# Pool's early block sums started by semaphore in VectorE's one-input stretches, with two splits and the late additions moved

## The chip, the cores and the metric

One Trainium2 chip, one core. The metric is the device time of one execution of the program, in microseconds (us). The core has five engines that run their own instruction streams and wait for one another by semaphores: TensorE (PE in the profile; its weight loads are PEld), VectorE (DVE), ScalarE (ACT), GpSimd (POOL) and SyncE (SP, whose queue issues the DMAs). SBUF is the on-chip memory, PSUM the accumulators that TensorE writes.

## The reference

A gated linear attention over 4 batches, 8 heads, 768 tokens and head size 48, followed by a mixture of 8 experts whose token weights are balanced by eight rounds of row and column scaling:

```
f = 1 / (1 + exp(-f_logit))
for t in range(768):
    state = f[:, :, t, :, None] * state + outer(k[:, :, t], v[:, :, t])
    y[:, :, t] = q[:, :, t] @ state
x = y as (3072, 384)
P = exp(x @ w_gate - max)
for _ in range(8):
    P /= P.sum(1) + 1e-09;  P /= P.sum(0) + 1e-09;  P *= 3072 / 8
out = sum over e of P[:, e] * (relu(x @ w1[e]) @ w2[e])      # 384 -> 1024 -> 384
```

## The kernel before

**Splits.** Every fp32 matrix is split into two fp16 parts, a high part (rounded by ScalarE) and a low part (the rest, by VectorE or Pool), and a product is three fp16 matmuls.

**Attention.** The work is cut into 24 items of 128 tokens, six for each batch; an item holds all heads on 112 partitions and 512 columns (8 blocks of 64 tokens). `item(i)` is a Python generator, and each `yield` ends a step. In each step the loop in `fast` lets every live item do its next piece and then lets TensorE do a fixed amount of filler work. A new item begins every 8 steps, so two items overlap. An item loads q, k and f (tile `q`) and v, and does in this order: a sigmoid (L728), a backward scan `r` (L735), the product of k with r (L750, two fp32 inputs in SBUF), the low part of v (`vlc`, L751), a forward scan (L753; one input `ft` in SBUF, the other, `pi`, in PSUM), its product with q on Pool (L760), the split of k (`kb`, L763 and L771) and of the q side (`qh` on ScalarE, L769; `ql` on Pool, L776), a DMA transpose of `kb`, the score matmuls `aps`, the masked scores `am` (L808) and their split `ah` (L814), `al` (Pool, L823), the state `st` and its split `sh` (L822), `sl` (L830, two inputs in SBUF), and the output matmuls `yps`, which read ah, al, qh, ql, sh and sl. The output is split into the token tiles `xh` and `xl`.

**The filler.** Between these pieces TensorE runs experts 0 and 1 directly on finished token tiles: `hps` (first layer), `hh`/`hl` (its split after the relu: ScalarE L470 or L423, VectorE L473 or L424), `yps` (second layer), `yr` (copy out, L494 or L441, then a store).

**The block sums.** After attention the other experts run in a scheme with 15 block products for each period; it needs sums of 128x256 blocks of x. For each batch a list of jobs does this: three additions x = xh + xl (kind V, L986), 17 block sums on Pool (P, L1000), three maxima (V, L1003), two copies (A, L1008), five high parts (H, `xah`/`xbh`, L1016) and five low parts (L, `xal`/`xbl`, L1021). For batches 0 and 1 the jobs run early, inside the items, by `hook`: from item 8 on for batch 0 and from item 15 on for batch 1, at most one VectorE job ahead of the forward scan, up to five Pool and copy jobs behind `td` (L756), and up to two high parts behind `al`. For batches 2 and 3 `convert` runs them beside the balancing of the token weights (`sinkhorn`: tiny VectorE steps, L140 to L172, with matmuls `sk_t`, `sk_m` and `sk_c` between).

**What sets the order.** `pin` chains the instructions of each engine in the order of the code, and `mm` does so for TensorE, so an engine never overtakes a waiting instruction. DMAs on the SP queue are placed by the scheduler.

Of the kernel before, what the change touches and what calls it, by code (L numbers as in the profile page):

```python
# [12 lines left out]
AF = mybir.ActivationFunctionType  # L13
ALU = mybir.AluOpType
# [21 lines left out]
SS = 2.0 ** -11  # L36
# [72 lines left out]
FIRSTAT = ((0,), (0,), (0, 4), (0, 7), (1, 9), (5, 10))  # L109
SECONDAT = ((16, 17), (18, 20), (17, 18), (17, 21), (20, 21), (20, 22), (24, 24), (24, 25))  # L110
CONVSTEP = (30,)
EARLY = {0: 8, 1: 15}
POOL_SUMS = 5
PUTOFF = 17
X_BY_POOL = ()
# [171 lines left out]
def fast(ctx, tc, qkf, vbd, wg, w1, w2, out, flag):  # L287
    nc = tc.nc
# [427 lines left out]
    def item(i):  # L716
# [32 lines left out]
        km = k.rearrange("r (n t) -> r n t", t=C)  # L749
        pin(nc.vector.scalar_tensor_tensor(out=km, in0=km, scalar=KS, in1=r3, op0=ALU.mult, op1=ALU.mult))  # L750
        pin(nc.vector.scalar_tensor_tensor(out=vlc, in0=vr, scalar=VS, in1=vhc, op0=ALU.mult, op1=ALU.subtract))  # L751
        hook(i, 'VL', 1)
        pin(nc.vector.tensor_tensor_scan(out=fl, data0=ft[:, 0:L], data1=pi.rearrange("r n t -> r (n t)"), initial=0.0, op0=ALU.mult, op1=ALU.add))  # L753
        if i == 3:
            pin(nc.vector.tensor_tensor(out=fl, in0=fl, in1=q, op=ALU.mult))
        pin(nc.gpsimd.tensor_tensor(out=td, in0=td, in1=r3[:, :, 0], op=ALU.mult))  # L756
        hook(i, 'PA', POOL_SUMS)
        yield
        if i > 3:
            pin(nc.gpsimd.tensor_tensor(out=fl, in0=fl, in1=q, op=ALU.mult))  # L760
# [5 lines left out]
        ql = ap.tile([R, L], F16, name=f"ql_{i}", tag="ql")  # L766
        for o, rs in vl:
            pin(nc.scalar.activation(out=o, in_=vlc[rs], func=AF.Copy))
        pin(nc.scalar.activation(out=qh, in_=fl, func=AF.Copy))  # L769
        for rs, ks in heads:  # L770
            pin(nc.gpsimd.tensor_tensor(out=kb[rs, 1, :, ks], in0=km[rs], in1=kb[rs, 0, :, ks], op=ALU.subtract))  # L771
        yield
        kt = ktb[i % 2][:, 0:2 * NB * R].rearrange("p (n r) -> p n r", r=R)
        nc.sync.dma_start_transpose(out=kt, in_=kb.rearrange("r n c s -> r (n c) s"))
        yield
        pin(nc.gpsimd.tensor_tensor(out=ql, in0=fl, in1=qh, op=ALU.subtract))  # L776
        yield from wait(4)
        st = ap.tile([R, CT, NP, D], F32, name=f"st_{i}", tag="st")
        td3 = td.rearrange("r (p c) -> r p c", c=CT)
        if s:  # L780
# [46 lines left out]
            pin(nc.vector.tensor_tensor(out=carry[b, s + 1], in0=kvps[1][0:R], in1=st[:, 1], op=ALU.add))  # L827
        yield
        for (o, rs), (hi, _) in zip(sl, sh):
            pin(nc.vector.scalar_tensor_tensor(out=o, in0=sf[rs], scalar=SS, in1=hi, op0=ALU.mult, op1=ALU.subtract))  # L830
        yield
        yield
        if not s:
# [145 lines left out]
    def jobs(b, pools):  # L979
        xqp, alloc, x32 = pools(b)  # L980
        eng = nc.gpsimd if b in X_BY_POOL else nc.vector
        xh, xl = xt[b]
        kept = {}

        def add(k):
            pin(eng.tensor_tensor(out=x32[k], in0=xh[:, k].rearrange("p u t -> p (u t)"), in1=xl[:, k].rearrange("p u t -> p (u t)"), op=ALU.add))  # L986

        def block(v):
            if isinstance(v, str):
                q = int(v[1])  # L990
                return x32[q // 3].rearrange("p (u t) -> p u t", u=2)[:, :, 128 * (q % 3):128 * (q % 3) + 128]
            n = XPOS.index(v)
            return kept['s'][n // 9][:, n % 9, :].rearrange("p (u t) -> p u t", u=2)

        def total(i):
            if not i:
                kept['b'] = [xqp.tile([128, 6, 256], F16, name=f"xb{n}{b}") for n in "hl"]
                kept['s'] = alloc()
            r, p, op, q = XSUMS[i]
            pin(nc.gpsimd.tensor_tensor(out=block(r), in0=block(p), in1=block(q), op=ALU.add if op == '+' else ALU.subtract))  # L1000

        def most(k):
            pin(nc.vector.tensor_reduce(out=xmx[:, b, k:k + 1], in_=x32[k], axis=AX.X, op=ALU.max, apply_absolute_value=True))  # L1003

        def one(n):
            r, q, sign = XONE[n]
            for src, dst in zip((xh, xl), kept['b']):
                pin(nc.scalar.activation(out=dst[:, 4 + n, :].rearrange("p (u t) -> p u t", u=2), in_=src[:, q // 3, :, 128 * (q % 3):128 * (q % 3) + 128], func=AF.Copy, scale=sign))  # L1008

        PIECES = [(0, 0, 3), (0, 3, 6), (0, 6, 9), (1, 0, 2), (1, 2, 4)]  # L1010

        def high(i):
            if not i:
                kept['a'] = [xp.tile([128, 9, 256], F16, name=f"xa{n}{b}", tag=f"x{n}{b}", bufs=1) for n in "hl"]
# [54 lines left out]
    def early_pools(b):
        x32 = [raw_tile(f"x32_{b}_{k}") for k in range(KT)]  # L1070
# [36 lines left out]
    for n in range(8):  # L1107
        at_steps(second[n], 4 + n, *SECONDAT[n])
    begin = {LEADS + STEPS * (i - 3): i for i in range(3, NT)}
    while live or g < max(begin):  # L1110
        if g == 2:
            third = early_item(2)
            go(third)
        if g == 6:
            go(third)
        if g == 9:
            live.append(third)
        if g + 4 in begin:
# [509 lines left out]
```

## Time and profile before

| | |
|---|---|
| time, median of 3 runs | 1482.09 us (1480.91 to 1482.21) |
| profiled execution | 1482.9 us, of it the span 1481.1 us |
| PE busy | 1442.2 us (97% of the span) |
| DVE, ACT, POOL busy | 1254.7, 1110.7, 1082.5 us |
| mean granted TensorE clock | 0.994 |

The items run from the start to about 370 us, the balancing to about 435 us, and the periods of block products fill the rest. PE's busy time can hide a slow clock: a matmul at half clock is busy twice as long. So two things are read together: the waits in front of PE's instructions, and the granted clock of each stretch.

### The profile page before, as it was taken

The numbers are of one execution on the slowest core, as the hardware profiler recorded it, in microseconds if no ns is written. First come the engines' busy times: TensorE is split into PE (matmuls) and PEld (weight loads), VectorE is DVE, ScalarE is ACT, GpSimd is POOL, SyncE is SP. The second block draws the span as 40 slices with busy tenths as digits, with TensorE's granted clock in tenths as the row PEclk, the third lists the DMA queues.
The fourth block names the chain that finished last, engine by engine and source line by source line (L and its number), as shares of the span: only waits on it lengthen the run. The fifth ranks groups of instructions, "written<-read, shape, count | busy, mean of one in ns | idle before, by whom it ended". The sixth has DMA issues, their size and how long they took to land.

```text
span 1481.1 us, 40831 instructions
## 1 busy us (share of the span) xinstructions
PE 1442.2 (97%) x16193; PEld 1268.5 (86%) x16193; DVE 1254.7 (85%) x2569; ACT 1110.7 (75%) x2492; POOL 1082.5 (73%) x1286
## 2 busy tenths in 40 slices
PE   7999999989999999999999999999999999999997
PEld 5778876656557999999999999999999999999996
DVE  8867888986687998899989888888888888888886
ACT  7767768676437778888888888888777777778774
POOL 3344664653454669999999999999888888888873
PEclk9999999999999999999999999999999999999999
DMA  8344435461101012222111111111000000000201
GB/s 261 89 107 128 121 96 126 106 153 49 49 22 60 12 29 61 61 56 60 53 49 58 55 42 47 50 55 50 23 23 23 23 23 23 12 21 14 81 7 67
DMA packets 82809, 90.53 MB, mean 61 GB/s; under 512 B 49872, under 2 KB 69456, under 8 KB 82608
## 3 DMA queue, kind: packets, MB, share of 16 engines
q1 hardware_dynamic: 82176, 87.25, 21.1%
q8 instruction: 128, 2.10, 0.6%
q14 instruction: 73, 0.60, 0.1%
q10 hardware_dynamic: 432, 0.59, 0.1%
HBM read 64.03 MB, written 14.16 MB: 53 GB/s over the span
## 4 chain that ended last, share of the span: by engine, by line
PE 73%; DVE 4%; ACT 0%; issue 0%; DVEq 0%; ACTq 0%
PE kyps L315 29%; PE kb_A L315 9%; PE kb_B L315 9%; PE kb_D L315 6%; PE kxps L315 5%; PE kb_C L315 4%; PE yps L315 4%; PE hps L315 3%; PE kb_E L315 2%; PE kb_F L315 2%; DVE x L986 0%; DVE k1l L1173 0%; DVE hl L424 0%; DVE acc L1329 0%; DVE xal L1021 0%
## 5 line engine op out<-in xcount | busy, mean ns | idle before, releaser
L315 PEld LDWEIGHTS <-k1h 128*128 128x128 f16 x3000 | 282.5, 98 | 21.9 <-issue 2.3
L315 PE MATMUL kyps<-k2h,kgh 128*128 128x192 f16 x1200 | 295.2, 246 | 1.5 <-ACT kyps L1326 1.5
L315 PE MATMUL kyps<-k2h,kgl 128*128 128x192 f16 x1200 | 295.2, 246 | 0.0
L315 PE MATMUL kyps<-k2l,kgh 128*128 128x192 f16 x1200 | 295.2, 246 | 0.0
L315 PEld LDWEIGHTS <-kgh 128*128 128x128 f16 x2400 | 220.9, 98 | 8.5 <-issue 1.8
L1501 POOL TENSOR_TENSOR kgl<-kf,kgh 128x512 f16<-128x512 f32 x147 | 197.3, 1342 | 2.1 <-ACT kgh L1498 2.1
L1329 DVE SCALAR_TENSOR_TENSOR yy<-kyps,pes,part 128x192 f32<-128x192 f32 x270 | 111.4, 413 | 94.6 <-PE kyps L315 84.3
L1501 POOL TENSOR_TENSOR kgl<-kr,kgh 128x512 f16<-128x512 f32 x147 | 174.1, 1184 | 9.6 <-PE kyps L315 8.2
L1368 POOL TENSOR_TENSOR acc<-acc,yy 128x384 f32<-128x384 f32 x135 | 135.0, 1000 | 57.7 <-DVE yy L1329 57.7
L315 PEld LDWEIGHTS <-k1l 128*128 128x128 f16 x1500 | 146.8, 98 | 17.1
L315 PEld LDWEIGHTS <-kh 128*128 128x128 f16 x1200 | 112.7, 98 | 8.4 <-issue 1.8
L315 PEld LDWEIGHTS <-kgl 128*128 128x128 f16 x1200 | 117.4, 98 | 0.1
L315 PE MATMUL yps<-w2h,hh 128*128 128x384 f16 x336 | 111.4, 332 | 5.0 <-ACT hh L470 3.1
L315 PE MATMUL yps<-w2h,hl 128*128 128x384 f16 x336 | 111.6, 332 | 2.3 <-DVE hl L473 2.2
L315 PE MATMUL yps<-w2l,hh 128*128 128x384 f16 x336 | 111.4, 332 | 0.6 <-DVE w2l L388 0.6
L315 PEld LDWEIGHTS <-w1h 128*128 128x128 f16 x1248 | 87.9, 98 | 27.8 <-issue 2.7
L315 PEld LDWEIGHTS <-hh 128*128 128x128 f16 x672 | 65.8, 99 | 44.4 <-ACT hh L470 3.9
L1452 ACT ACTIVATE cp<-kb_A 128x512 f32<-128x512 f32 x150 | 89.8, 599 | 18.1 <-DVE kb_A L1454 15.5
L1326 ACT ACTIVATE kyps<-kyps 128x192 f32<-128x192 f32 x150 | 48.2, 321 | 67.8 <-PE kyps L315 65.7
L1498 ACT ACTIVATE kgh<-kf 128x512 f16<-128x512 f32 x150 | 94.9, 633 | 0.5 <-DVE kf L1475 0.4
L1498 ACT ACTIVATE kgh<-kr 128x512 f16<-128x512 f32 x150 | 94.3, 628 | 0.0
L1478 POOL TENSOR_TENSOR kr<-kr 128x256 f32<-128x256 f32 x100 | 75.9, 759 | 22.6 <-ACT kr L1467 20.4
(320 smaller groups left out, 5382.5 us busy)
## 6 DMA issues: line engine op xcount, KB each, us to landing
q<-in_qkf_dram SPq DMA_DIRECT2D x23, 672.0 KB, 5.4
k1r<-in_w_dram SPq DMA_DIRECT2D x26, 384.0 KB, 3.0
k2r<-in_w_dram SPq DMA_DIRECT2D x26, 384.0 KB, 3.0
ys<-yr SPq DMA_DIRECT2D x48, 192.0 KB, 2.3
yb<-ys SPq DMA_DIRECT2D x48, 192.0 KB, 2.3
vr<-in_vbd_dram SPq DMA_DIRECT2D x24, 192.0 KB, 2.5
out_dram<-acc SPq DMA_DIRECT2D x21, 192.0 KB, 1.9
w1r<-in_w_dram SPq DMA_DIRECT2D x8, 384.0 KB, 7.4
```

The lines of the kernel that those rows point to most:

```text
L315: ins = (nc.tensor.transpose if transpose else nc.tensor.matmul)(**kw)
L1326: pin(nc.scalar.activation(out=out, in_=in_, func=AF.Copy, **kw))
L1329: pin(nc.vector.scalar_tensor_tensor(out=y, in0=ps, scalar=p, in1=z, op0=ALU.mult, op1=ALU.add))
L1368: pin(nc.gpsimd.tensor_tensor(out=y, in0=y, in1=z.rearrange("p s d -> p (s d)"), op=ALU.add))
L1452: pin(nc.scalar.activation(out=fresh(ev[2]), in_=bk, func=AF.Copy))
L1478: pin((nc.gpsimd if ev[2] == 'P' else nc.vector).tensor_tensor(out=r[:, 0], in0=r[:, 1], in1=r[:, 0], op=ALU.subtract))
L1498: pin(nc.scalar.activation(out=hs['g', t][0][i], in_=hs['f' if i else 'r', t], func=AF.Copy))
L1501: pin((nc.vector if tag == str(PERIODS - 1) else nc.gpsimd).tensor_tensor(out=hs['g', t][1][i], in0=hs['f' if i else 'r', t], in1=hs['g', ...
```

## The change

Four edits. (1) The first Pool sum of a hook gets a semaphore dependency on a VectorE instruction (`turn`): in front of the forward scan one sum waits for the last VectorE instruction ahead of that scan; up to three jobs (P, A or V) move behind `sl`, the first sum of them waiting for the last `sl`. The maxima move there too. (2) `qh` is issued one step later, behind the transpose DMA, and `ql` one step later; the score matmuls stay in their step. (3) The additions of batches 2 and 3 (now kind X) take one step each. (4) Batch 1 starts its early jobs at item 16, and what is left of the early jobs runs two at a time in the steps after the last item has begun its second half.

```
--- before.py
+++ after.py
@@ -109,7 +109,7 @@
 FIRSTAT = ((0,), (0,), (0, 4), (0, 7), (1, 9), (5, 10))
 SECONDAT = ((16, 17), (18, 20), (17, 18), (17, 21), (20, 21), (20, 22), (24, 24), (24, 25))
 CONVSTEP = (30,)
-EARLY = {0: 8, 1: 15}
+EARLY = {0: 8, 1: 16}
 POOL_SUMS = 5
 PUTOFF = 17
 X_BY_POOL = ()
@@ -749,12 +749,13 @@
         km = k.rearrange("r (n t) -> r n t", t=C)
         pin(nc.vector.scalar_tensor_tensor(out=km, in0=km, scalar=KS, in1=r3, op0=ALU.mult, op1=ALU.mult))
         pin(nc.vector.scalar_tensor_tensor(out=vlc, in0=vr, scalar=VS, in1=vhc, op0=ALU.mult, op1=ALU.subtract))
-        hook(i, 'VL', 1)
+        hook(i, 'XVL', 1)
+        turn = last.get(mybir.EngineType.DVE)
         pin(nc.vector.tensor_tensor_scan(out=fl, data0=ft[:, 0:L], data1=pi.rearrange("r n t -> r (n t)"), initial=0.0, op0=ALU.mult, op1=ALU.add))
         if i == 3:
             pin(nc.vector.tensor_tensor(out=fl, in0=fl, in1=q, op=ALU.mult))
         pin(nc.gpsimd.tensor_tensor(out=td, in0=td, in1=r3[:, :, 0], op=ALU.mult))
-        hook(i, 'PA', POOL_SUMS)
+        hook(i, 'PA', 1, turn)
         yield
         if i > 3:
             pin(nc.gpsimd.tensor_tensor(out=fl, in0=fl, in1=q, op=ALU.mult))
@@ -766,15 +767,16 @@
         ql = ap.tile([R, L], F16, name=f"ql_{i}", tag="ql")
         for o, rs in vl:
             pin(nc.scalar.activation(out=o, in_=vlc[rs], func=AF.Copy))
-        pin(nc.scalar.activation(out=qh, in_=fl, func=AF.Copy))
         for rs, ks in heads:
             pin(nc.gpsimd.tensor_tensor(out=kb[rs, 1, :, ks], in0=km[rs], in1=kb[rs, 0, :, ks], op=ALU.subtract))
         yield
         kt = ktb[i % 2][:, 0:2 * NB * R].rearrange("p (n r) -> p n r", r=R)
         nc.sync.dma_start_transpose(out=kt, in_=kb.rearrange("r n c s -> r (n c) s"))
+        pin(nc.scalar.activation(out=qh, in_=fl, func=AF.Copy))
+        yield
         yield
         pin(nc.gpsimd.tensor_tensor(out=ql, in0=fl, in1=qh, op=ALU.subtract))
-        yield from wait(4)
+        yield from wait(3)
         st = ap.tile([R, CT, NP, D], F32, name=f"st_{i}", tag="st")
         td3 = td.rearrange("r (p c) -> r p c", c=CT)
         if s:
@@ -827,7 +829,8 @@
             pin(nc.vector.tensor_tensor(out=carry[b, s + 1], in0=kvps[1][0:R], in1=st[:, 1], op=ALU.add))
         yield
         for (o, rs), (hi, _) in zip(sl, sh):
-            pin(nc.vector.scalar_tensor_tensor(out=o, in0=sf[rs], scalar=SS, in1=hi, op0=ALU.mult, op1=ALU.subtract))
+            turn = pin(nc.vector.scalar_tensor_tensor(out=o, in0=sf[rs], scalar=SS, in1=hi, op0=ALU.mult, op1=ALU.subtract))
+        hook(i, 'PAV', 3, turn)
         yield
         yield
         if not s:
@@ -997,7 +1000,10 @@
                 kept['b'] = [xqp.tile([128, 6, 256], F16, name=f"xb{n}{b}") for n in "hl"]
                 kept['s'] = alloc()
             r, p, op, q = XSUMS[i]
-            pin(nc.gpsimd.tensor_tensor(out=block(r), in0=block(p), in1=block(q), op=ALU.add if op == '+' else ALU.subtract))
+            ins = pin(nc.gpsimd.tensor_tensor(out=block(r), in0=block(p), in1=block(q), op=ALU.add if op == '+' else ALU.subtract))
+            if gated[0]:
+                tc.add_manual_dep(ins.ins, gated[0].ins.name, mybir.DependencyInfo(mybir.DependencyClass.Sync, mybir.DependencyReason.DATA), reason="port turn")
+                gated[0] = None
 
         def most(k):
             pin(nc.vector.tensor_reduce(out=xmx[:, b, k:k + 1], in_=x32[k], axis=AX.X, op=ALU.max, apply_absolute_value=True))
@@ -1023,7 +1029,7 @@
                 xc[b] = [[(kept['a'] if n < 9 else kept['b'])[q][:, n % 9, :] for n in range(PRODUCTS)] for q in range(2)]
 
         for k in range(KT):
-            yield 'V', lambda k=k: add(k)
+            yield 'X', lambda k=k: add(k)
         for i in range(len(XSUMS)):
             yield 'P', lambda i=i: total(i)
             if i in (1, 5, 9):
@@ -1041,7 +1047,7 @@
             while kind == 'H' and raw_left() > 0:
                 yield
             job()
-            if kind in 'PL':
+            if kind in 'PLX':
                 yield
 
     class Early:
@@ -1057,14 +1063,16 @@
                 self.next = next(self.jobs, None)
                 most -= 1
 
-    early = {}
-
-    def hook(i, kinds, most):
+    early, gated = {}, [None]
+
+    def hook(i, kinds, most, after=None):
+        gated[0] = after
         for b, first in EARLY.items():
             if i >= first:
                 if b not in early:
                     early[b] = Early(b)
                 early[b].run(kinds, most)
+        gated[0] = None
 
     def early_pools(b):
         x32 = [raw_tile(f"x32_{b}_{k}") for k in range(KT)]
@@ -1107,6 +1115,7 @@
     for n in range(8):
         at_steps(second[n], 4 + n, *SECONDAT[n])
     begin = {LEADS + STEPS * (i - 3): i for i in range(3, NT)}
+    begin_tail = max(begin) + 17
     while live or g < max(begin):
         if g == 2:
             third = early_item(2)
@@ -1125,9 +1134,12 @@
         put_off[0] = g < PUTOFF
         fill([n for at_, n in FILL if g >= at_][-1])
         go_all(g)
+        if g > begin_tail:
+            for run in early.values():
+                run.run('AHLVP', 2)
         g += 1
     for run in early.values():
-        run.run('AHLPV', 99)
+        run.run('AHLPVX', 99)
     actx.close()
     xq = ctx.enter_context(tc.tile_pool(name="xq", bufs=1, reuse_waits="tile"))
     accp = ctx.enter_context(tc.tile_pool(name="accp", bufs=B, reuse_waits="tile"))
```

TensorE's instructions stand in the same order before and after. Pool's order at items 12 and 13, `q_12` and `q_13` being the items' q tiles and `xs` the block sums, before:

```order
L771 TENSOR_TENSOR kb_124<-q_12_3630,kb_124 48x8x64 x2
L776 TENSOR_TENSOR ql_3938<-q_12_3630,qh_3937 112x512
L823 TENSOR_TENSOR al_4011<-am_3977,ah_4010 128x512
L756 TENSOR_TENSOR tds<-tds,r_4058 112x8
L1000 TENSOR_TENSOR xs_0_3208<-x_0_0_2603,x_0_2_2605 128x256
L1000 TENSOR_TENSOR xs_0_3207<-xs_0_3207 128x256
L1000 TENSOR_TENSOR xs_0_3208<-x_0_2_2605,x_0_0_2603 128x256
L1000 TENSOR_TENSOR xs_0_3207<-xs_0_3207 128x256
L1000 TENSOR_TENSOR xs_0_3207<-xs_0_3207,x_0_0_2603 128x256
L760 TENSOR_TENSOR q_13_3944<-q_13_3944 112x512
```

and after, at the same place:

```order
L771 TENSOR_TENSOR kb_124<-q_12_3625,kb_124 48x8x64 x2
L825 TENSOR_TENSOR al_4006<-am_3971,ah_4005 128x512
L778 TENSOR_TENSOR ql_3933<-q_12_3625,qh_3932 112x512
L1003 TENSOR_TENSOR xs_0_3207<-x_0_1_2604,xs_0_3207 128x256
L1003 TENSOR_TENSOR xs_0_3207<-x_0_0_2603,x_0_1_2604 128x256
L757 TENSOR_TENSOR tds<-tds,r_4057 112x8
L1003 TENSOR_TENSOR xs_0_3207<-x_0_0_2603,x_0_1_2604 128x256
L761 TENSOR_TENSOR q_13_3938<-q_13_3938 112x512
```

Ahead of item 13's product with q (L760, now L761) stands one sum instead of five, behind its `td` (L756, now L757); two others stand ahead of `td`, behind `ql`, and `al` of the item before stands ahead of `ql`. ScalarE's order in item 12, before:

```order
L768 ACTIVATE vl_140<-vlc_3767 64x8x48 x2
L769 ACTIVATE qh_3937<-q_12_3630 112x512
L470 ACTIVATE hh_2_1_0_3959<-hps_2_1_0_3851 128x512
L470 ACTIVATE hh_2_1_1_4004<-hps_2_1_1_3963 128x512
L814 ACTIVATE ah_4010<-am_3977 128x512
```

and after:

```order
L769 ACTIVATE vl_140<-vlc_3768 64x8x48 x2
L470 ACTIVATE hh_2_1_0_3953<-hps_2_1_0_3846 128x512
L775 ACTIVATE qh_3932<-q_12_3625 112x512
L470 ACTIVATE hh_2_1_1_3999<-hps_2_1_1_3957 128x512
L816 ACTIVATE ah_4005<-am_3971 128x512
```

`qh` has moved behind the filler's `hh` of the next unit. VectorE's order in the balancing, where batch 3's additions (`x_3`) stand, before:

```order
L172 TENSOR_TENSOR pe<-pe,sk_cs 128x192
L1173 SCALAR_TENSOR_TENSOR k1l_0_7700<-k1s_0_7613,k1h_0_7699 128x640
L986 TENSOR_TENSOR x_3_7743<-xh_5948,xl_5949 128x768 x3
L159 TENSOR_REDUCE pe<-pe 128x24
L160 TENSOR_SCALAR sk_rs<-pe 128x24
L161 RECIPROCAL sk_rs<-sk_rs 128x24
L1173 SCALAR_TENSOR_TENSOR k1l_0_7700<-k1s_0_7613,k1h_0_7699 128x640
L163 TENSOR_TENSOR pe<-pe,sk_rs 128x192
L164 TENSOR_REDUCE sk_cs<-pe 128x8
```

and after:

```order
L172 TENSOR_TENSOR pe<-pe,sk_cs 128x192
L1185 SCALAR_TENSOR_TENSOR k1l_0_7700<-k1s_0_7608,k1h_0_7699 128x640
L989 TENSOR_TENSOR x_3_7743<-xh_5941,xl_5942 128x768
L159 TENSOR_REDUCE pe<-pe 128x24
L160 TENSOR_SCALAR sk_rs<-pe 128x24
L161 RECIPROCAL sk_rs<-sk_rs 128x24
L1185 SCALAR_TENSOR_TENSOR k1l_0_7700<-k1s_0_7608,k1h_0_7699 128x640
L989 TENSOR_TENSOR x_3_7743<-xh_5941,xl_5942 128x768
L163 TENSOR_TENSOR pe<-pe,sk_rs 128x192
L164 TENSOR_REDUCE sk_cs<-pe 128x8
```

One addition instead of three stands between the scaling of `pe` (L172) and the row sums (L159, one line in both), and a second one between the reciprocal (L161) and L163.

## Rows read from the trace of the kernel before

**Rows 1.** The page, busy time of each engine.
```profile
PE 1442.2 (97%) x16193; PEld 1268.5 (86%) x16193; DVE 1254.7 (85%) x2569; ACT 1110.7 (75%) x2492; POOL 1082.5 (73%) x1286
```
**Rows 2.** Waits of PE, 74 to 480 us: total, times, longest.
```profile
PE yps L315 <- ACT hh L470: 2.9, 2, 2.7
PE sk_c L315 <- DVE sk_cs L164: 2.4, 2, 2.1
PE yps L315 <- POOL al L823: 2.2, 2, 1.1
PE yps L315 <- DVE hl L473: 2.0, 5, 0.7
PE lps L315 <- DVE am L808: 2.0, 3, 1.1
PE yps L315 <- ACT hh L423: 1.6, 1, 1.6
PE sk_t L315 <- DVE sk_sm L140: 1.4, 1, 1.4
PE sk_m L315 <- DVE sk_r L146: 0.9, 1, 0.9
...
```
**Rows 3.** Two windows: PE, PEld, DVE, ACT, POOL busy, granted clock, DMA, GB/s.
```profile
190.00:200.00 10.00, 7.13 (x56) 4.18 (x54) 7.23 (x17) 5.30 (x12) 6.41 (x7) 0.83 0.58 138
420.00:430.00 10.00, 7.92 (x40) 4.16 (x39) 9.66 (x22) 2.18 (x6) 7.67 (x12) 0.83 0.13 41
```
**Rows 4.** Groups (74 to 360 us: busy, mean ns | idle), then timeline rows (start, duration).
```profile
L750 DVE SCALAR_TENSOR_TENSOR q<-q,r 112x512 f32<-112x512 f32 x19 | 30.1, 1585 | 0.0
...
L753 DVE TENSOR_TENSOR_SCAN q<-ft,pib 112x512 f32<-112x512 f32 x19 | 22.9, 1208 | 0.0
...
142.57 0.67 DVE L750 SCALAR_TENSOR_TENSOR q<-q,r 112x512 f32<-112x512 f32 x1
...
199.59 3.97 DVE L750 SCALAR_TENSOR_TENSOR q<-q,r 112x512 f32<-112x512 f32 x1
...
202.27 0.74 POOL L1000 TENSOR_TENSOR xs<-xs,x 128x256 f32<-128x256 f32 x1
```
**Rows 5.** Timeline, a forward scan with Pool sums beside it.
```profile
157.44 1.21 DVE L753 TENSOR_TENSOR_SCAN q<-ft,pib 112x512 f32<-112x512 f32 x1
157.59 0.72 POOL L1000 TENSOR_TENSOR xs<-x,x 128x256 f32<-128x256 f32 x1 [2.10 <-DVE x L986]
```
**Rows 6.** Timeline of ScalarE in front of PE's longest wait.
```profile
191.52 0.63 ACT L769 ACTIVATE qh<-q 112x512 f16<-112x512 f32 x1 [1.38 <-POOL q L760]
...
192.17 1.08 ACT L470 ACTIVATE hh<-hps 128x512 f16<-128x512 f32 x2
```
**Rows 7.** Timeline of Pool, `ql` of one item and `al` of the item before.
```profile
311.50 1.35 POOL L776 TENSOR_TENSOR ql<-q,qh 112x512 f16<-112x512 f32 x1
312.81 1.47 POOL L823 TENSOR_TENSOR al<-am,ah 128x512 f16<-128x512 f32 x1
```
**Rows 8.** Timeline of ScalarE, two high parts of batch 1.
```profile
324.95 1.58 ACT L1016 ACTIVATE xah<-xs 128x768 f16<-128x768 f32 x2
```
**Rows 9.** Timeline of VectorE in the balancing.
```profile
382.33 2.68 DVE L986 TENSOR_TENSOR x<-xh,xl 128x768 f32<-128x768 f16 x3
...
419.56 2.69 DVE L986 TENSOR_TENSOR x<-xh,xl 128x768 f32<-128x768 f16 x3
```
**Rows 10.** Timeline of `al`, `sl` and PE's reading of `sl` in two items.
```profile
195.86 1.29 DVE L830 SCALAR_TENSOR_TENSOR sl<-st,sh 48x384 f16<-48x384 f32 x2 [0.65 <-ACT sh L822]
...
201.31 0.40 PE L315 MATMUL yps<-qh,sl 112*128 112x64 f16 x8
...
239.95 1.16 POOL L823 TENSOR_TENSOR al<-am,ah 128x512 f16<-128x512 f32 x1
240.23 2.08 DVE L830 SCALAR_TENSOR_TENSOR sl<-st,sh 48x384 f16<-48x384 f32 x2 [0.20 <-ACT sh L822]
...
242.62 0.40 PE L315 MATMUL yps<-qh,sl 112*128 112x64 f16 x8
```

More of the change, by code (lines that the diff above doesn't have):

```diff
@@ L111 @@
 CONVSTEP = (30,)
-EARLY = {0: 8, 1: 15}
+EARLY = {0: 8, 1: 16}
 POOL_SUMS = 5
@@ L751, in item @@
         pin(nc.vector.scalar_tensor_tensor(out=vlc, in0=vr, scalar=VS, in1=vhc, op0=ALU.mult, op1=ALU.subtract))
-        hook(i, 'VL', 1)
+        hook(i, 'XVL', 1)
+        turn = last.get(mybir.EngineType.DVE)
         pin(nc.vector.tensor_tensor_scan(out=fl, data0=ft[:, 0:L], data1=pi.rearrange("r n t -> r (n t)"), initial=0.0, op0=ALU.mult, op1=ALU.add))
@@ L756, in item @@
         pin(nc.gpsimd.tensor_tensor(out=td, in0=td, in1=r3[:, :, 0], op=ALU.mult))
-        hook(i, 'PA', POOL_SUMS)
+        hook(i, 'PA', 1, turn)
         yield
@@ L768, in item @@
             pin(nc.scalar.activation(out=o, in_=vlc[rs], func=AF.Copy))
-        pin(nc.scalar.activation(out=qh, in_=fl, func=AF.Copy))
         for rs, ks in heads:
@@ L774, in item @@
         nc.sync.dma_start_transpose(out=kt, in_=kb.rearrange("r n c s -> r (n c) s"))
+        pin(nc.scalar.activation(out=qh, in_=fl, func=AF.Copy))
+        yield
         yield
         pin(nc.gpsimd.tensor_tensor(out=ql, in0=fl, in1=qh, op=ALU.subtract))
-        yield from wait(4)
+        yield from wait(3)
         st = ap.tile([R, CT, NP, D], F32, name=f"st_{i}", tag="st")
@@ L829, in item @@
         for (o, rs), (hi, _) in zip(sl, sh):
-            pin(nc.vector.scalar_tensor_tensor(out=o, in0=sf[rs], scalar=SS, in1=hi, op0=ALU.mult, op1=ALU.subtract))
+            turn = pin(nc.vector.scalar_tensor_tensor(out=o, in0=sf[rs], scalar=SS, in1=hi, op0=ALU.mult, op1=ALU.subtract))
+        hook(i, 'PAV', 3, turn)
         yield
@@ L999, in total @@
             r, p, op, q = XSUMS[i]
-            pin(nc.gpsimd.tensor_tensor(out=block(r), in0=block(p), in1=block(q), op=ALU.add if op == '+' else ALU.subtract))
+            ins = pin(nc.gpsimd.tensor_tensor(out=block(r), in0=block(p), in1=block(q), op=ALU.add if op == '+' else ALU.subtract))
+            if gated[0]:
+                tc.add_manual_dep(ins.ins, gated[0].ins.name, mybir.DependencyInfo(mybir.DependencyClass.Sync, mybir.DependencyReason.DATA), reason="port turn")
+                gated[0] = None
         def most(k):
@@ L1025, in jobs @@
         for k in range(KT):
-            yield 'V', lambda k=k: add(k)
+            yield 'X', lambda k=k: add(k)
         for i in range(len(XSUMS)):
@@ L1043, in convert @@
             job()
-            if kind in 'PL':
+            if kind in 'PLX':
                 yield
@@ L1058, in run, with hook @@
                 most -= 1
-    early = {}
-    def hook(i, kinds, most):
+    early, gated = {}, [None]
+    def hook(i, kinds, most, after=None):
+        gated[0] = after
         for b, first in EARLY.items():
@@ L1067, in hook @@
                 early[b].run(kinds, most)
+        gated[0] = None
     def early_pools(b):
@@ L1109, in fast @@
     begin = {LEADS + STEPS * (i - 3): i for i in range(3, NT)}
+    begin_tail = max(begin) + 17
     while live or g < max(begin):
@@ L1127, in fast @@
         go_all(g)
+        if g > begin_tail:
+            for run in early.values():
+                run.run('AHLVP', 2)
         g += 1
     for run in early.values():
-        run.run('AHLPV', 99)
+        run.run('AHLPVX', 99)
     actx.close()
```

## The prediction

> **What bounds the kernel now.** I read the page's busy times first: TensorE is busy for 1442.2 us of a span of 1481.1 us, 97%, and no other engine is over 85% [rows 1]. So time can come only from TensorE's own gaps and from stretches in which its clock is low. Its instructions stand in the same order after the change, so its work is the same and only its waits can move. The second view is the list of TensorE's waits in the stretch that the change touches, 74 to 480 us. It has thirteen rows; the eight largest add up to 15.4 us and the other five to 2.1, together 17.5 us [rows 2]. The reader is to see that none is large: the longest single wait is 2.7 us, and most are for the splits of the filler (`hh`, `hl`), for `al` and `am`, and for the balancing's tiny steps. The third view is the table of windows: in the whole stretch the granted clock fell twice, to 0.83 as a mean of 190 to 200 us and of 420 to 430 us [rows 3]. The two levels are 2.4 and 1.2 GHz, so a mean of 0.83 over 10 us means 3.4 us at the lower one, in which half, 1.7 us of work, was lost. In the same two windows TensorE is idle for 2.9 and 2.1 us, its two longest waits. All that the change can win is therefore 17.5 + 2 x 1.7 = 20.9 us, and the lowest time is 1482.9 - 20.9 = 1462.0 us.
>
> **Part 1, the sums in VectorE's one-input turns.** L750 multiplies two fp32 tiles in SBUF. Undisturbed it takes 0.67 us; beside the five Pool sums of item 13 it takes 3.97 us and ends only when the last sum, begun at 202.27 us and 0.74 us long, is over [rows 4]. The 19 of them between 74 and 360 us take 30.1 us instead of 19 x 0.67 = 12.7: 17.4 us of VectorE are spent waiting for Pool. The forward scan, which reads one input from SBUF and one from PSUM, takes 1.21 us with sums beside it [rows 5], and 1208 ns as a mean of all 19 [rows 4]. The change starts one sum (0.72 us) as that scan starts, and up to three behind `sl`, where a scan and steps on PSUM follow. The sum ends inside the scan, and the product with q that is queued behind it waits for the scan anyway; so this wait costs nothing, and if the sum were to outlast the scan it would cost 0.72 - 1.21 < 0, nothing again. Behind the sums at `sl` stand `st` and `td` of later items; nearly a whole item (eight steps) passes until they are read.
>
> The Trainium skill (SBUF — State Buffer, Who interferes with whom) says that a VectorE instruction with two SBUF inputs and a GpSimd instruction that reads SBUF exclude each other, and that whichever begins first holds the shared ports for that instruction. The first half agrees with the 3.97 and 1.21 us above [rows 4, 5]. The second would let L750 in after one sum, at about 0.74 + 0.67 = 1.41 us; the trace has 3.97, so sums without a pause between them keep VectorE out for all of them. By the page the edit would be worth far less VectorE time; I take the trace.
>
> What of the 17.4 us reaches TensorE? The chain behind L750 is the scan, Pool's product, `qh`, and then, because ScalarE keeps its order, `hh`. At 191.52 us `qh` had waited 1.38 us for Pool's product, `hh` began only at 192.17 us, and TensorE waited 2.7 us [rows 2, 6]. Part 2 puts that `hh` ahead of `qh`. Either edit alone removes this wait. Together I take the whole `hh` row of L470, 2.9 us; half of the five `hl` waits of L473, 1.0; of the 2.0 us for `am`, which queues behind L750 and the scan on VectorE, 1.7 [rows 2]; and the first fall of the clock, 1.7 [rows 3]. Sum 7.3 us. Bounds: nothing, if VectorE has other work there; or all three rows and the clock, 8.6 us. I stand near the upper end because the 17.4 us are twice what TensorE waited.
>
> **Part 2, qh and ql a step later.** `al` now goes ahead of `ql` on Pool. In the rows, `ql` takes 1.35 us and `al` starts behind it [rows 7]; TensorE's two waits for `al` are 1.1 us each, less than a `ql` [rows 2]. Both go: 2.2 us. The new cost: `al` and `ql` now run back to back, and `sl`, with two SBUF inputs, must wait for the pair instead of for `al` alone. `al` is 1.16 us long and kept an `sl` pair busy for 2.08 us; TensorE read it 0.3 us after its end; in another item the pair took 1.29 us and TensorE came 4.2 us later [rows 10]. So the cover is between 0.3 and 4.2 us, and a `sl` held for a `ql`, which has the shape of `al` and so its 1.16 us, costs between 0 and 1.16 - 0.3 = 0.9 us an item. With 20 items behind the third the bounds are 0 and 18 us; I take 1.5, near the lower end, because the cover is short only where VectorE was late, and VectorE becomes earlier. Transposes, loads and stores in the SP queue that wait for Pool move by at most this step; each is used about an item later, and I cost them at nothing. Uncovered, one `ql` more, 1.35 us each time.
>
> **Part 3, batch 1 an item later.** The two high parts `xah` (1.58 us) [rows 8] stood ahead of an `hh`, and TensorE's one wait for L423, 1.6 us, is as long [rows 2]. In the new order they stand behind the last item's `sh`, ahead of a copy out, which nothing waits for at once. 1.6 us, bounds 0 and 1.6.
>
> **Part 4, later additions one per step.** Ahead of the balancing's first steps, the low parts of batch 1 leave the place in front of L140; TensorE's 1.4 us for `sk_t` should become about 0.3. Two additions (1.8 us) instead of three (2.68) [rows 9] stand ahead of the step that `sk_m` needs, and TensorE, too, arrives earlier; of its 0.9 us I let 0.4 stay. That is 1.6 us. At 419.56 us three additions cost 2.69 us between `pe` and the sums for `sk_c` [rows 9]; the new order leaves two there, so the wait of 2.1 us falls by 0.9 to 1.2, and the next `sk_c` waits some 0.3 more, while the small one (2.4 - 2.1 = 0.3) goes. Gain 0.9 us. A wait of 1.6 us is in the rows without a fall of the clock in its window, so I expect none at 1.2: 1.7 us more [rows 2, 3]. Together 4.2 us; bounds 0.9 (only one addition less) and 2.4 + 1.4 + 0.9 + 1.7 = 6.4.
>
> **The sum.** 7.3 + 2.2 + 1.6 + 4.2 = 15.3 us. Off go 1.5 for `sl`, and 1.1 that I set aside for new waits: the maxima (L1003) now stand ahead of an `hl`, and a TensorE that comes earlier meets suppliers that the gaps had hidden. Net 12.7 us: 1482.9 - 12.7 = 1470.2 us. The profiled execution is 0.8 us above the median of the runs, which would give 1469.4; I forecast **1470**.
>
> **Rivals.**
> - *The pair lets sl in between.* If VectorE gets its turn between `al` and `ql`, the 1.5 us is not paid: 1468.7 us. For it speaks only the page's sentence above, by which the ports are held for one instruction; against it the 3.97 us [rows 4]. Chance 0.10.
> - *Half of it comes back.* The clock falls once more at the shorter `sk_c` wait (1.7), the two `xah` delay another `hh` (1.6), and `sl` costs 4.0 instead of 1.5 (0.5 us in eight items). 12.7 - 1.7 - 1.6 - 2.5 = 6.9: 1476.0 us. For it: the short cover of 0.3 us [rows 10]; against it: each needs VectorE or ScalarE to stay as late as now. Chance 0.20.
> - *It does not do what it says.* Only the first sum of a hook waits; up to two follow it freely. If they run into the next L750, the stretch remains, and `al` is all that is won: 1482.9 - 2.2 = 1480.7 us. Against it: a scan of 1.2 us and further steps stand between `sl` and L750. Chance 0.07.
> - *The pair holds sl everywhere.* If the cover is 0.3 us in each of 20 items, the cost is 20 x 0.9 = 18 us against a gain of 15.3 - 1.1 = 14.2: 1482.9 + 3.8 = 1486.7 us. It decides from 14.2 / 20 = 0.7 us an item. For it: nothing hands the ports over inside a run of Pool instructions [rows 4]; against it: the cover of 4.2 us in one item [rows 10]. Chance 0.06.
>
> **How the numbers follow.** My forecast has 0.57; its own range, with the terms of parts 1 and 4 between their middle and their upper ends, is 1466 to 1474. The range that is to hold the time 8 times in 10 takes in the first two rivals: 1465.5 to 1477. No change is within 0.2% (3 us, 1479.1 to 1485.1), about what a measurement of this kernel can tell. Faster takes the forecast and the first two rivals, 0.87; the third lies within, 0.07; slower 0.06.
>
> **What would show it.** In the new profile: L750 at 0.7 us in all items, no wait for `al`, `hh` (L470) or `am` over 0.5 us between 74 and 340 us, the clock at 1.00 in both windows where it fell, `sk_t` under 0.5 and the long `sk_c` wait near 1.2 us. The forecast is wrong if L750 is still stretched, if waits for `sl` or `hl` add up to more than 4 us, or if the clock falls in a new place, which costs 1.7 us each time.

## The result and the profile after

The changed kernel takes 1466.03 us (median of four runs, 1465.98 to 1466.08) against 1482.15 us, a ratio of 0.9892 (95% interval 0.9875 to 0.9909): 16.1 us faster. The forecast was 1470, the range 1465.5 to 1477. The page of the new profile, busy time of each engine; its span is 1464.3 us:

```profile
PE 1435.2 (98%) x16193; PEld 1266.4 (86%) x16193; DVE 1243.3 (85%) x2569; ACT 1111.9 (76%) x2492; POOL 1084.9 (74%) x1286
```

TensorE is still the bound, with the same 16193 matmuls [rows 1]. Its waits between 74 and 464 us, which is the work of 74 to 480 us in the kernel before, the answer to [rows 2] (total, times, longest):

```profile
PE sk_c L315 <- DVE sk_cs L164: 3.2, 3, 1.2
PE yps L315 <- DVE hl L473: 0.7, 1, 0.7
PE yps L315 <- DVE hl L424: 0.6, 1, 0.6
PE kb_B L315 <- ACT cp L1464: 0.5, 1, 0.5
PE kvb L315 <- DVE kvb L795: 0.3, 1, 0.3
PE kb_touchk L315 <- DVE pes L1151: 0.3, 1, 0.3
PE yps L315 <- DVE sl L832: 0.3, 1, 0.3
PE sk_t L315 <- DVE sk_sm L140: 0.3, 1, 0.3
PE yps L315 <- ACT hh L423: 0.2, 1, 0.2
```

They add up to 6.4 us, against 17.5. The waits for `al`, `am`, `sk_m` and the `hh` of L470 are gone, four of five `hl` of L473 too. Three rows grew or are new: `sk_c`, from 2.4 us in two waits to 3.2 us in three; the `hl` of L424 in front of `yps`, 0.6 instead of 0.2, at another place; and `kb_touchk`, 0.3. The two windows of [rows 3], in the same columns, show full clock (the work that stood behind the second fall now runs at about 408 to 411 us; from 30 to 1440 us the new profile has no fall at all):

```profile
190.00:200.00 10.00, 10.00 (x195) 8.74 (x194) 7.15 (x12) 8.03 (x19) 7.65 (x9) 1.00 0.66 156
420.00:430.00 10.00, 9.09 (x56) 5.19 (x54) 8.29 (x17) 4.10 (x9) 9.16 (x11) 1.00 0.04 6
```

VectorE's groups between 74 and 345 us (busy, mean ns | idle), to be read beside [rows 4]:

```profile
L832 DVE SCALAR_TENSOR_TENSOR sl<-st,sh 48x384 f16<-48x384 f32 x34 | 29.0, 853 | 4.1 <-ACT sh L824 3.7
...
L754 DVE TENSOR_TENSOR_SCAN q<-ft,pib 112x512 f32<-112x512 f32 x19 | 23.0, 1210 | 0.0
...
L750 DVE SCALAR_TENSOR_TENSOR q<-q,r 112x512 f32<-112x512 f32 x19 | 12.9, 681 | 0.0
```

L750 fell from 1585 to 681 ns, the scan stayed. How the turns look in one item, VectorE first and then Pool (start, duration, idle before):

```profile
190.91 0.66 DVE L832 SCALAR_TENSOR_TENSOR sl<-st,sh 48x384 f16<-48x384 f32 x1 [0.65 <-ACT sh L824]
191.59 1.41 DVE L832 SCALAR_TENSOR_TENSOR sl<-st,sh 48x384 f16<-48x384 f32 x1
...
194.82 0.67 DVE L750 SCALAR_TENSOR_TENSOR q<-q,r 112x512 f32<-112x512 f32 x1
...
195.87 1.21 DVE L754 TENSOR_TENSOR_SCAN q<-ft,pib 112x512 f32<-112x512 f32 x1
```
```profile
190.00 1.15 POOL L825 TENSOR_TENSOR al<-am,ah 128x512 f16<-128x512 f32 x1 [1.31 <-ACT ah L816]
191.11 1.47 POOL L778 TENSOR_TENSOR ql<-q,qh 112x512 f16<-112x512 f32 x1
193.08 0.73 POOL L1003 TENSOR_TENSOR xs<-x,xs 128x256 f32<-128x256 f32 x1 [0.49 <-DVE sl L832]
...
196.03 0.72 POOL L1003 TENSOR_TENSOR xs<-x,x 128x256 f32<-128x256 f32 x1 [1.23 <-DVE vlc L751]
197.16 1.26 POOL L761 TENSOR_TENSOR q<-q 112x512 f32<-112x512 f32 x1 [0.41 <-DVE q L754]
...
217.68 1.16 POOL L778 TENSOR_TENSOR ql<-q,qh 112x512 f16<-112x512 f32 x1
```

Two sums wait for `sl` (0.49 us) and run beside VectorE's next scan; one waits for `vlc` (1.23 us) and lies inside the forward scan. The product with q then waits 0.41 us for the scan, not for the sum. `sl` is two instructions, one for each half. The first ends at 191.56, 0.4 us after `al` (191.15) and long before the end of `ql`; the second ends at 193.00, 0.4 us after `ql` (192.58). `ql` takes 1.47 us here, and 1.16 in an item where no `sl` comes in front of it (last line).

As TensorE's order is the same in both kernels, the starts of equal matmuls can be subtracted. The lead of the new kernel, by the time in the kernel before:

| time before (us) | 74 | 192 | 197 | 207 | 271 | 296 | 328 | 386 | 424 | 429 | 446 | 1400 |
|---|---|---|---|---|---|---|---|---|---|---|---|---|
| lead (us) | 0.4 | 4.6 | 6.4 | 7.3 | 8.7 | 11.5 | 15.4 | 17.3 | 16.7 | 18.3 | 17.0 | 16.8 |

So the items give 15.4 us, 1.8 of it from 192 to 197, the first clock fall with a 0.2 us wait for `hl` in it. The balancing wins 1.9 (`sk_t`, `sk_m`), loses 0.7 net between the new `sk_c` waits and the long one that shrank, wins 1.7 by the second clock fall and loses 1.4 behind it. The late stages change nothing.

### The profile page after: what moved, and what is told of

Same layout as the page of the kernel before. It is cut to its first block, busy times and chain, and to the rows that moved or that the text cites. A ratio compares the mean times of both kernels' runs of the same rounds, so it can differ in the third digit from the quotient of the medians.

```text
span 1464.3 us, 40830 instructions
## 1 busy us (share of the span) xinstructions
PE 1435.2 (98%) x16193; PEld 1266.4 (86%) x16193; DVE 1243.3 (85%) x2569; ACT 1111.9 (76%) x2492; POOL 1084.9 (74%) x1286
## 4 chain that ended last, share of the span: by engine, by line
PE 71%; DVE 3%; issue 2%; POOL 2%; ACT 1%; DVEq 0%; POOLq 0%; ACTq 0%
PE kyps L315 29%; PE kb_A L315 9%; PE kb_B L315 9%; PE kb_D L315 6%; PE kxps L315 5%; PE kb_C L315 4%; PE yps L315 3%; PE kb_E L315 2%; PE kb_F L315 2%; PE hps L315 1%; POOL xs L1003 1%; POOL k1s L1173 1%; DVE k1l L1185 0%; DVE yy L1341 0%; DVE acc L1341 0%
```

## The experiments

Each was timed beside the kernel before, whose median lay between 1482.27 and 1482.95 us; "under the kernel before" is against that median. "Over the changed kernel" is against its 1466.03 us, which were measured apart, so a few tenths of a us there are not told apart by the times alone.

**Does the wait itself matter, or the place?** The order of each compute engine stays; Pool no longer waits for the turn.

```diff
-        hook(i, 'PA', 1, turn)
+        hook(i, 'PA', 1)
...
-        hook(i, 'PAV', 3, turn)
+        hook(i, 'PAV', 3)
```


> The changed kernel with every instruction in the same place on every engine, but Pool's sums no longer wait for VectorE's turn: one sum is still issued beside the forward scan and up to three behind sl. Theory (the wait itself keeps the two engines apart): a sum now begins while L750 or sl runs; L750 goes from a mean of 681 ns to about 1.4 us (one sum of 0.73 us in most of the 19 items, 10 to 14 us of VectorE), sl gets longer by one to three sums where they are issued, and 2 to 5 us of waits for hl, am or sl come back: 1468 to 1471 us. Rival (only the placement counts, since no five sums stand together any more): L750 under 0.9 us and 1466.0 us within 1.

Measured: 1466.53 us (ratio 0.9895, 0.9879 to 0.9910), 0.5 over the changed kernel. VectorE's groups, same view as above:

```profile
L832 DVE SCALAR_TENSOR_TENSOR sl<-st,sh 48x384 f16<-48x384 f32 x34 | 35.5, 1044 | 4.1 <-ACT sh L824 3.7
...
L750 DVE SCALAR_TENSOR_TENSOR q<-q,r 112x512 f32<-112x512 f32 x19 | 15.2, 802 | 0.0
```

The collisions come back, but small: L750 121 ns more, `sl` 191 ns more. The rival is nearer: spreading the sums is nearly all of part 1, and the semaphore is worth about 0.5 us, which is little enough to be uncertain; the trace has one new wait, 0.14 us for `sl`, at which 0.3 us is lost.

**Part 1 undone.**

```diff
-        hook(i, 'PA', 1, turn)
+        hook(i, 'PA', POOL_SUMS)
...
-        hook(i, 'PAV', 3, turn)
```


> The changed kernel with part 1 undone: five Pool sums at a time beside L750, no waits by semaphore, nothing issued at sl; qh and ql, batch 1 and the later additions as in the change. Theory: L750 is back at a mean near 1.6 us; the waits for hl and am come back, 2.0 and 1.7 us, but the wait for hh of 2.7 us and the clock fall at 193 us stay away, because hh now stands ahead of qh: 1466.0 + 2.5 to 4.5 = 1468.5 to 1470.5 us. Rival (the stretch alone causes all four): hh and the clock come back too, 1466.0 + 7.3 = about 1473.3 us.

Measured: 1474.60 us (0.9954, 0.9940 to 0.9967), 8.6 over the changed kernel; the rival is nearer. Its group, two TensorE starts behind waits, and the window (columns as before):

```profile
L750 DVE SCALAR_TENSOR_TENSOR q<-q,r 112x512 f32<-112x512 f32 x19 | 29.9, 1576 | 0.0
```
```profile
189.57 0.34 PE L315 MATMUL yps<-w2h,hh 128*128 128x384 f16 x1 [0.92 <-ACT hh L470]
191.04 0.50 PE L315 MATMUL yps<-w2h,hl 128*128 128x384 f16 x1 [0.97 <-DVE hl L473]
```
```profile
190.00:200.00 10.00, 9.03 (x117) 6.41 (x116) 9.16 (x13) 5.35 (x11) 7.83 (x10) 0.83 0.57 134
```

`hh` does come earlier with part 2, but `hl`, VectorE's own work, still queues behind the stretched L750; the wait is split in two and the clock falls all the same.

**Part 2 undone.**

```diff
+        pin(nc.scalar.activation(out=qh, in_=fl, func=AF.Copy))
         for rs, ks in heads:
...
-        pin(nc.scalar.activation(out=qh, in_=fl, func=AF.Copy))
-        yield
         yield
         pin(nc.gpsimd.tensor_tensor(out=ql, in0=fl, in1=qh, op=ALU.subtract))
-        yield from wait(3)
+        yield from wait(4)
```


> The changed kernel with part 2 undone: qh and ql where they stood before, all else as in the change. Theory: the two waits for al of 1.1 us each come back and nothing else, since L750 is no longer stretched: 1466.0 + 2.2 to 2.6 = about 1468.4 us. Rival (the place of qh alone keeps the wait for hh away): that wait (2.9) and the clock fall (1.7) come back as well, about 1473 us.

Measured: 1468.50 us (0.9907, 0.9892 to 0.9923), 2.5 over. The number is the theory's, the place is not: there is no wait for `al`. TensorE instead waits a little twice at each of four places, one of which is here; at three of them the kernel before waits alike. Then Pool in a late item:

```profile
67.78 0.34 PE L315 MATMUL yps<-w2h,hh 128*128 128x384 f16 x1 [0.28 <-ACT hh L470]
68.50 0.34 PE L315 MATMUL yps<-w2h,hl 128*128 128x384 f16 x1 [0.23 <-DVE hl L473]
```
```profile
299.00 1.35 POOL L777 TENSOR_TENSOR ql<-q,qh 112x512 f16<-112x512 f32 x1
300.31 1.47 POOL L824 TENSOR_TENSOR al<-am,ah 128x512 f16<-128x512 f32 x1
```

`al` is still behind `ql`, and ends at 301.78 us, but TensorE reads it at 302.79; in the kernel before it ended at 314.28 and was read at 314.33. Pool's product waits for the scan behind L750, so a short L750 should bring the whole Pool chain forward; here `al` is covered by 1.0 us. That L750 alone does it is not shown: part 3 alone, below, removes the other of the two `al` waits while L750 is still stretched. What part 2 still wins is `qh` (0.63 us) out of the way of `hh` and `hl`.

**Part 2 alone**, the same lines put into the kernel before.

> The kernel before with part 2 alone: qh and ql a step later, the five sums, batch 1 and the later additions as before. Theory: the waits for al (2.2) and for hh of L470 (2.9) and the clock fall at 193 us (1.7) go, L750 stays stretched, its mean near 1.6 us: 1482.1 - 6.8 = about 1475.3 us, if sl, held by al and ql together, costs nothing. Rival (the pair costs sl what was set aside, 1.5): 1476.8. Second rival (hh comes late by L750 whatever the order): only al goes, 1479.9 us.

Measured: 1479.25 us (0.9981, 0.9972 to 0.9990), 3.2 under the kernel before: nearest the second rival in time, but in no theory's way. VectorE, then TensorE, then two windows:

```profile
197.62 3.95 DVE L750 SCALAR_TENSOR_TENSOR q<-q,r 112x512 f32<-112x512 f32 x1
...
203.95 1.26 DVE L473 SCALAR_TENSOR_TENSOR hl<-hps,hh 128x512 f16<-128x512 f32 x2
```
```profile
204.67 0.50 PE L315 MATMUL yps<-w2h,hl 128*128 128x384 f16 x1 [2.56 <-DVE hl L473]
```
```profile
190.00:200.00 10.00, 9.04 (x145) 7.43 (x144) 9.14 (x14) 6.83 (x15) 7.83 (x10) 1.00 0.60 126
200.00:210.00 10.00, 7.44 (x89) 4.82 (x87) 7.84 (x13) 4.67 (x10) 6.38 (x7) 0.83 0.23 60
```

The waits for `al` go. The long `hh` becomes an `hh` of 0.94 and an `hl` of 0.96 us, behind which the clock stays up, and soon after an `hl` of 2.56 us with a clock fall stands right behind a stretched L750. Reordering ScalarE and Pool cannot help where the late engine is VectorE.

**Part 3 alone**, in the kernel before.

```diff
-EARLY = {0: 8, 1: 15}
+EARLY = {0: 8, 1: 16}
```


> The kernel before with part 3 alone: batch 1 begins an item later; what is left of it after the items runs in one go ahead of the balancing, as before. Theory of the prediction: the wait for hh of L423 (1.6 us) goes, all else stays: 1482.1 - 1.6 = about 1480.5 us. Rival (with the sums five at a time the delayed pieces pile up ahead of the balancing): sk_t waits longer than 1.4 us and the time is 1482 to 1485 us.

Measured: 1479.36 us (0.9979, 0.9970 to 0.9988), 2.9 under the kernel before. Waits of TensorE, 74 to 480 us:

```profile
PE sk_t L315 <- DVE sk_sm L140: 2.2, 1, 2.2
...
PE yps L315 <- POOL al L823: 1.1, 1, 1.1
...
PE yps L315 <- ACT hh L423: 0.6, 1, 0.6
...
PE lps L315 <- DVE am L808: 0.4, 1, 0.4
```

Both theories hold in part: `hh` falls from 1.6 to 0.6, and `sk_t` grows from 1.4 to 2.2; but most of `am` and one `al` go as well, so the parts share waits. (The change without part 3 was not tried.)

**Part 4 without the pieces at the end of the items.**

```diff
-        if g > begin_tail:
-            for run in early.values():
-                run.run('AHLVP', 2)
```


> The changed kernel without the new pieces at the end of the items: what is left of batch 1's low parts (xal three times, xbl twice) runs in one go ahead of the balancing again; the later additions stay one per step. Theory of the prediction (the low parts ahead of L140 made the sk_t wait of 1.4 us): that wait comes back, longer by the later start of batch 1, 1.4 to 2.2 us instead of 0.3, and little else: 1466.0 + 1.1 to 2.0 = 1467 to 1468 us. Rival (the low parts are covered by the filler's matmuls wherever they stand): 1466.0 within 0.5.

Measured: 1470.39 us (0.9917, 0.9903 to 0.9930), 4.4 over the changed kernel. TensorE's start behind the wait, and the window after it:

```profile
368.88 0.37 PE L315 MATMUL sk_t<-identf,sk_sm 128*1 128x128 f32 x1 [3.10 <-DVE sk_sm L140]
```
```profile
370.00:380.00 10.00, 10.00 (x58) 5.92 (x57) 5.52 (x14) 4.71 (x9) 7.68 (x12) 0.91 0.11 39
```

The theory's wait, but 3.1 us long instead of 1.4 to 2.2, and with a clock fall of its own. In the changed kernel these pieces are worth 4.4 us; with them `sk_t` is 0.3.

**Part 4 without the additions one per step.**

```diff
-            if kind in 'PLX':
+            if kind in 'PL':
```


> The changed kernel with the additions of batches 2 and 3 three in one step again (half of part 4 undone; the low parts of batch 1 stay in their new place). The prediction's theory: the sk_c wait near 417 us grows by the one addition that is more, 0.9 us, and the clock falls there again, 1.7 us, and sk_m gets back some 0.4: 1466.0 + 2.6 to 3.0 = about 1469 us. Rival, from the two traces (one long wait and a clock fall have only become three sk_c waits, 3.2 us in all, of the same cost): 1466.0 to 1467.5 us.

Measured: 1465.82 us (0.9892, 0.9877 to 0.9907): no difference from the changed kernel, but its four times are two near 1465.0 and two near 1466.5; the profiled one is 1465.17. The long wait is back, and the window around it:

```profile
408.14 0.39 PE L315 MATMUL sk_c<-sk_cs,onesf 128*128 128x8 f32 x2 [2.08 <-DVE sk_cs L164]
```
```profile
404.00:416.00 12.00, 9.92 (x62) 5.78 (x61) 11.07 (x27) 2.69 (x7) 10.01 (x16) 1.00 0.15 51
```

This wait is as long as the one at 424 us in the kernel before, and here the clock did not fall. The additions one per step gain nothing: 2.4 us of `sk_c` and 0.9 of `sk_m` here stand against 3.2 of `sk_c`, 0.6 of `hl` and 0.3 of `kb_touchk` there. These last two waits are in every run here that spreads the additions evenly, and not in this one.

**Is sl's hold paid?** `ql` one step later still. By the traces it then holds the second half of `sl` in six items between 74 and 345 us instead of nine.

```diff
         yield
         yield
+        yield
         pin(nc.gpsimd.tensor_tensor(out=ql, in0=fl, in1=qh, op=ALU.subtract))
-        yield from wait(3)
+        yield from wait(2)
```


> The changed kernel with ql one more step later (qh stays), so that al and ql no longer stand back to back on Pool and sl is held by al alone. Theory (what al and ql together add to sl, a mean of 853 ns instead of 740, is covered by VectorE's slack): 1466.0 us within 0.6, with a lower mean for sl. Rival (the 1.5 us that the prediction set aside for it is really paid): 1464.5 us. Second rival (ql comes too late for the product with q): TensorE waits for ql, over 1468 us.

Measured: 1466.00 us (0.9892, 0.9876 to 0.9907). The mean of `sl` falls from 853 to 799 ns and nothing else moves: the theory. The hold is real and, where this edit lifts it, covered.

**A better version.** What is left is `sk_c`, three waits. In front of the first, at 393.36 us, two low parts of batch 2 stand between L172 and L164. In front of the second, at 400.51 us, VectorE is late already at L168, where it takes up TensorE's column sums, because two more low parts and two splits of the filler stand behind L164 (the maximum of `k1r` that follows stands there in the kernel before too, with a wait of 0.1 us):

```profile
393.22 0.95 DVE L1027 TENSOR_TENSOR xal<-xs,xah 128x768 f16<-128x768 f32 x1
...
394.55 0.68 DVE L1027 TENSOR_TENSOR xbl<-xs,xbh 128x512 f16<-128x512 f32 x1
```

VectorE in front of the third, and TensorE's start behind it:

```profile
402.76 0.37 DVE L172 TENSOR_TENSOR pe<-pe,sk_cs 128x192 f32<-128x192 f32 x1
403.04 0.81 DVE L1185 SCALAR_TENSOR_TENSOR k1l<-k1s,k1h 128x640 f16<-128x640 f32 x1
403.77 0.95 DVE L989 TENSOR_TENSOR x<-xh,xl 128x768 f32<-128x768 f16 x1
...
405.47 0.76 DVE L1185 SCALAR_TENSOR_TENSOR k1l<-k1s,k1h 128x640 f16<-128x640 f32 x1
406.14 0.94 DVE L989 TENSOR_TENSOR x<-xh,xl 128x768 f32<-128x768 f16 x1
...
407.40 0.36 DVE L164 TENSOR_REDUCE sk_cs<-pe 128x8 f32<-128x192 f32 x1
```
```profile
407.81 0.39 PE L315 MATMUL sk_c<-sk_cs,onesf 128*128 128x8 f32 x2 [1.21 <-DVE sk_cs L164]
```

3.5 us of side work stand between L172 and L164. Behind L164, where VectorE waits for TensorE, they should cost nothing as long as they fit into that wait:

```diff
-        for gen in list(work):
-            if next(gen, work) is work:
-                work.remove(gen)
+        for _ in range(1 if step < 6 else (0, 2, 2, 1, 0)[(step - 6) % 5]):
+            for gen in list(work):
+                if next(gen, work) is work:
+                    work.remove(gen)
```


> The changed kernel with the side work of the balancing (additions and maxima of batches 2 and 3, their low parts, k1l) put only where VectorE waits for TensorE's column sums: of each iteration's five steps two carry two pieces each, right behind L164, one carries one, two carry none. Theory (the three sk_c waits of 0.8 to 1.2 us are side work between L172 and L164): they fall under 0.3 us each and 2.5 to 3.5 us are won: about 1463 us, with no clock fall. Rival (the side work is only moved against the splits of the filler, whose hl then come late, and ScalarE's high parts in pairs delay hh): 1466 to 1468 us.

Measured: 1463.75 us (0.9877, 0.9862 to 0.9892), 2.3 under the changed kernel, nearer the theory than the rival. Its waits that differ, beside `kb_touchk` and the `hl` of 0.6, which are gone:

```profile
PE sk_c L315 <- DVE sk_cs L164: 1.5, 2, 1.2
PE hps L315 <- DVE hl L424: 0.8, 2, 0.5
```

Half of `sk_c` is gone; one wait of 1.2 us is left, after four low parts in a row, and 0.8 us for `hl` came in. A last kernel takes four pieces an iteration, (0, 2, 1, 1, 0).

> The kernel that put the side work behind L164, with four pieces an iteration instead of five (two, one, one). Theory: the one long sk_c wait left there, 1.2 us behind 3.1 us of low parts in a row, splits up and falls under 0.5; 1463.75 - 0.7 to 1.2 = about 1462.8 us. Rival (the side work ends later, and k1l comes late for the first matmuls of the next stage): waits of 1 us and more behind 425 us, 1464 us and over.

Measured: 1463.95 us (0.9873, 0.9858 to 0.9888), no difference from five pieces.

```profile
PE sk_c L315 <- DVE sk_cs L164: 1.4, 2, 0.9
```

The wait of 1.2 us went and the 0.8 for `hl` too, but the work only moved on: two later `sk_c` waits of 0.5 and 0.9 us, 0.9 for `kl` (L1519) and 0.5 for `kb_C` came. This is nearest the rival.

## Why the prediction was right, point by point

- **The bound.** Right. Listed waits went from 17.5 to 6.4 us. These 11.1 us and two falls of 1.7 make 14.5 of the 16.9 us between the two profiled executions (1482.9 and 1466.0); 0.4 was there before 74 us, and most of the rest is the first point of the last section. The floor, 1462.0 us, was meant with every wait gone, but left these hidden parts out: the changed kernel still lists 6.4 us of waits at 1466.0, so without them it would already be at 1459.6.
- **Part 1, forecast 7.3 with qh.** The mechanism is right (L750 at 0.68 us, the scan untouched), though the spreading does it and hardly the semaphore; the size is too small: undoing it costs 8.6 us. By the starts of equal matmuls, 2.5 of them are lost at waits for the `hh` and `hl` of L423 and L424, which the sum had put in part 3. The term left half of the `hl` waits of L473; four of five go, but three of about 0.2 us go by part 2, as the run without part 2 has them still, and by part 1 the one of 0.7. "Either edit alone removes this wait" is half right: without part 1 the long `hh` becomes an `hh` and an `hl` of 0.9 and 1.0 us with the same clock fall.
- **Part 2, forecast 2.2.** Right in size (2.5), wrong in place: the `al` waits go by the other parts too. What it alone wins is `qh` out of the way of `hh` and `hl`.
- **sl held by the pair, 1.5.** Wrong in how it is held, and the price was 0, the lower bound: one wait of 0.3 us for `sl`, as there was one of 0.7 in the kernel before. It is not held for `al` and `ql` together. Its first half gets its turn when `al` ends, `ql` takes 0.31 us longer for it, and only the second half is held by `ql`. So of the rival by which the ports change hands between `al` and `ql` the mechanism came true, and not its price: the 1.5 us were nowhere to be paid. The Trainium skill (SBUF — State Buffer, Who interferes with whom) speaks of one instruction; that is what the two halves of `sl` show, and not what L750 shows beside five sums (3.97 us). The 2.08 us of [rows 10] were misread too: they are two halves as well, of which the second ended at 242.30 us, 0.4 after an `st` on Pool of 0.82 us (241.06) and not after `al`.
- **Part 3, 1.6.** In time it was worth more alone (2.9), and it shares waits with parts 1 and 2; in the changed kernel it stands with the end-of-item pieces of part 4, without which 4.4 us come back.
- **Part 4, forecast 4.2.** The step that failed. `sk_t` and `sk_m` went as said (1.9 by the lead). The long `sk_c` wait did become 1.2, but the additions spread over more steps push the low parts of batch 2 later, and two more waits of 0.8 and 1.2 us arose behind them; behind the balancing came 0.3 and 0.6 us more. The table of leads shows the balancing worth 1.6 us in all (17.0 - 15.4), with the clock fall in it; three additions at a time do as well.
- **New waits, 1.1 set aside.** Right in size, not in kind: behind the balancing TensorE now waits 0.3 us for `kb_touchk` and 0.6 for an `hl` of L424, where it did not wait before (1.4 us of lead). They come of part 4's additions, not of the maxima.
- **The sum.** 11.1 forecast for parts 1 to 3 against 15.4 measured, 4.2 for part 4 against 1.6; nothing was paid for `sl`, where 1.5 was set aside. The errors partly cancel, 1470 against 1466.0, so that the time lies in the range is in part luck.

## What to carry to other kernels

Look which instruction of a chain the delayed engine executes itself: moving others around it only moves the wait, as part 2 alone showed. Give an engine's side work the steps in which it waits for the bounding engine anyway, not equal shares of every step, and no more than fits there: that was worth 2.3 us more. And count gains of several edits together: undone or done one at a time, these parts share their waits and do not add up.

## What was not expected of the hardware

- Pool let VectorE in between some of its instructions and not between others. Between `al` and `ql` it did in every item of the changed kernel where an `sl` met them; between two block sums of the kernel before it never did, so that L750 ended 0.55 us after the last of up to five. In the run with `ql` one more step later L750 itself got in behind `ql`: 1.00 us at 194.32, and the small `tds` behind it took 1.12 us instead of 0.21. What makes the difference no run shows.
- A wait costs TensorE more than the trace lists. At the two `al` waits of 1.1 us the lead grew by 1.26 us each. The matmuls there start 0.03 us apart and are listed with 0.19 us each, so the modelled end of the last one hides 0.16 us of the wait; most of the other waits that went hide 0.16 or 0.17 too. With eleven waits fewer (22 times in the list before, 11 now) that makes, as an estimate, 1.8 us, most of the 2.0 that the listed waits, the falls and the start leave open.
- The granted clock does not follow from the size of a wait alone. It fell (0.83) behind waits of 0.92 and 0.97 us close together with part 1 undone and stayed at 1.00 behind 0.94 and 0.96 at the same matmuls with part 2 alone; it fell behind 2.1 us of `sk_c` in the kernel before [rows 2, 3] and not behind 2.08 at the same matmul with three additions. A forecast should give such a fall a chance, not a yes or no.
- The changed kernel's four times lie within 0.1 us, while fifteen of the kernel before spread over 4.2 (1480.65 to 1484.84), and the four with three additions fall in two groups (1464.92 and 1465.17, 1466.48 and 1466.62) about one clock fall apart. That the falls make this spread is likely. The mean clock that is noted with every execution bears it out for the kernel before: at 0.996 those fifteen took 1480.65 to 1481.89 us, at 0.994 or 0.995 1482.03 to 1483.22, at 0.993 1484.84. For the three additions it does not (0.996 for all four), and only one execution of each was profiled.
